# Three six-tile passes instead of four in a second network, with preparation work moved earlier

## The chip, the cores and the metric

The kernel runs on one core of a Trainium2 chip. The time is device microseconds for one execution. Three runs of the kernel before took 825.73 to 828.0 us, median 827.82 us.

## What is computed

Sparse attention (4 batches, 8 heads, 576 tokens, head size 64) gives 2304 tokens of 512 numbers. They go through a gated layer of eight experts, each token through one, and then through a second network that is the same for all tokens:

```python
h = np.maximum(x[mask] @ w1[e], 0.0)            # 512 -> 1024, per expert
out[mask] = gate_w[mask, None] * eom[mask, e, None] * (h @ w2[e])
...
h = np.maximum(x @ w_in, 0.0)                   # 512 -> 2048, all tokens
return (h * h @ w_out).astype(np.float32)       # 2048 -> 512
```

`w_in` and `w_out` arrive as float64, so the kernel must turn pairs of 32-bit words into float32 itself.

## The kernel before

**Every product is made of three.** Each float32 matrix is split into a high part (a copy rounded to fp32r, on ScalarE) and a low part (the difference, on VectorE). `mm3` (L936 to 939) multiplies high by high (L937) and the two mixed pairs (L938, L939; which line is which depends on the order of the arguments) into the same PSUM tile. In names an h stands for high and an l for low: `hw`/`lw` are weights of the experts, `xh`/`xl` tokens, `hh`/`hl` hidden values of an expert, `gh`/`gl` hidden values of the second network, `hwa`, `hwb`, `hwo` and `lwa`, `lwb`, `lwo` its weights.

**Stages.** Attention and routing end 180 us into the span. Then come eight experts, k = 0 to 7, with 416 tokens at first and 256 at last. Each has eight steps f. Step f makes one hidden block `h` (`e_l1`, 12 matmuls) and, two steps later, adds that block to the four output tiles `y` (`e_l2`, 12 matmuls). After step 7 ScalarE copies the four `y` into `y2T` (L1060), which holds the inputs of the second network. VectorE makes `hl` at L1037.

**The second network** goes over the 18 token tiles (128 tokens each) in passes. A pass with two halves uses seven products instead of eight per 256 hidden columns: `m_unit` forms products of combined weights (A11, A12, A22, S1 to S4; rows show m_0A and m_0S for unit 0) with sums of token blocks (B11, T1 to T4 and so on, made by `split2` in four parts, 0 to 3; its rows are L1082 `xt`, `xs` and L1066 `xh`/`xl`/`xbl`). Each product goes to one of only two PSUM buffers, and VectorE empties it: L1239 makes a running sum `u`, L1157 a sum `rl`. ScalarE then does Relu (L1159), Square (L1160) and the high part (L1065), VectorE the low part `gl` (L1066). `down` multiplies these by `hwo`/`lwo` into six output tiles `o`; `quarters` hands out that work in four pieces, which `m_unit` puts between the next unit's products. After the last unit of a pass each tile `o` is scaled (L1183 or L1185) and written by GpSimd as a scatter to `out` (L1186). Before, the passes cover 6, 6, 4 and 2 tiles; the last one has one half and uses `m_plain` (L937 rows `m<-xh,hwi`), with plain blocks of the weights.

**Conversion of float64.** `conv` (L184 to 198) takes 128 x 512 pairs: ScalarE takes the absolute value of the high word (L184), VectorE shifts and masks it (L186, L187) and scales the low word (L191, output `cvd`), GpSimd adds the two (L192, output `cvt`), VectorE puts the sign back (L198). It runs 16 times for `w_in` during the experts (tiles `e6`, `eo`; L993 then makes the combined weights `sa`, `sb`, which GpSimd writes to `ws_d`) at steps listed in `CONV`, and 16 times for `w_out` inside the first pass (loads `s0wo`, `s1wo`, result `rwo`).

**What sets the order.** The kernel is written in program order, and a scheduler with its own time estimates reorders instructions of each engine. On the chip each engine then takes its own list strictly in that order, so an instruction that waits holds up all that stand behind it.

The lines the change touches:

Of the kernel before, what the change touches and what calls it, by code (L numbers as in the profile page):

```python
# [7 lines left out]
F32 = mybir.dt.float32  # L8
# [3 lines left out]
U32 = mybir.dt.uint32  # L12
AF = mybir.ActivationFunctionType
ALU = mybir.AluOpType
# [6 lines left out]
P = 128  # L21
NT = B * S
D = H * HD
KD = D // P
E = 8
# [34 lines left out]
C0 = LATE * P // E  # L60
HB = 8

MG = [(3, 3), (3, 3), (2, 2), (2,)]
LPOOL = (13, 14, 15, 16, 17)
DS = 6
LN = 6
# [10 lines left out]
BLK = {n: i for i, n in enumerate("A21 A11 A22 A12 S1 S2 S3 S4".split())}  # L77
BW = 2 * P

CONV = [(k, f) for k in range(1, 8) for f in range(8)][2:-6]  # L80
NW = (max(CAPS) + P - 1) // P
NEG = -1.0e9

# [48 lines left out]
def moe_kernel(ctx, tc, q, k, v, wg, wog, w1, w2, w_in64, w_out64, consts, out, dbg=None):  # L132
# [48 lines left out]
    def conv(pool, raw, o, nm, parts_=False):  # L181
        hi, lo = raw[:, :, 1], raw[:, :, 0]
        n = hi.shape[1]
        nc.scalar.activation(o, hi.bitcast(F32), AF.Abs)  # L184
        t = pool.tile([P, n], I32, name=f"cvt{nm}", tag="cvt")
        nc.vector.tensor_scalar(t, hi, 3, 0x3FFFFFFF, op0=ALU.logical_shift_left, op1=ALU.bitwise_and)  # L186
        nc.vector.scalar_tensor_tensor(  # L187
            out=t, in0=hi, scalar=-0x40000000, in1=t, op0=ALU.bitwise_and, op1=ALU.bitwise_or
        )
        rd = pool.tile([P, n], I32, name=f"cvd{nm}", tag="cvd", bufs=1)  # L190
        nc.vector.tensor_scalar(rd, lo.bitcast(U32), 2.0**-29, None, op0=ALU.mult)  # L191
        nc.gpsimd.tensor_tensor(t, t, rd, op=ALU.add)  # L192
        if parts_:
            return t
        conv_end(t, o)
# [662 lines left out]
    raws = early[0]  # L858
    for g in range(len(MG)):
        for c in range(F2 // UC):  # L860
            units += [("wa", g, c), ("wb", g, c), ("wo", g, c)] if len(MG[g]) == 2 else [("wi", g, c), ("wo", g, c)]
    ready = {}
    nraw = [1]
    nwh = [-1]
# [2 lines left out]
    def prep_unit(u):  # L867
        kind, k, c = u
        cs = slice(c * UC, (c + 1) * UC)
        if kind == "w1":  # L870
            shp = [P, KD, UC]
        elif kind in ("wa", "wi"):
            shp = [P, 4, BW]
        elif kind == "wb":
            shp = [P, 3, BW]
        else:
            shp = [P, UC // P, D]
# [7 lines left out]
        if kind == "w1":  # L885
            src = w1[bass.ds(order_of(k), 1), :, cs].rearrange("e (a p) f -> p (e a) f", p=P)
        elif kind == "w2":
            src = w2[bass.ds(order_of(k), 1), cs, :].rearrange("e (a p) f -> p (e a) f", p=P)
        elif kind == "wi":
            src = ws_d[c, :, : 4 * BW].rearrange("p (b f) -> p b f", f=BW)  # L890
        elif kind == "wa":
            src = ws_d[c, :, BW : 5 * BW].rearrange("p (b f) -> p b f", f=BW)
        elif kind == "wb":
            src = ws_d[c, :, 5 * BW :].rearrange("p (b f) -> p b f", f=BW)
        else:
            src = wout_d[cs, :].rearrange("(a p) f -> p a f", p=P)
# [144 lines left out]

    ybk = {}

    def e_l2(k, f, hh, hl):
        C = CAPS[k]
        c, i = f * P // UC, f % (UC // P)
        wh, wl = get(("w2", k, c))
        if f == 0:
            ybk[k] = [psm.tile([P, 512], F32, name=f"y{k}_{d}", tag="a", bufs=6) for d in range(KD)]
        for d in range(KD):  # L1050
            ds_ = slice(d * P, (d + 1) * P)
            mm3(
                ybk[k][d][:, :C], wh[:, i, ds_], wl[:, i, ds_], hh[:, :C], hl[:, :C], f == 0, f == NF1 - 1
            )
        if f == NF1 - 1:
            off = 0
            if k:
                off = nc.values_load(meta[0:1, E + k : E + k + 1], engines=[ET.Activation], min_val=0, max_val=NT)
            for d in range(KD):
                nc.scalar.activation(y2T[:, d, bass.ds(off, C)], ybk[k][d][:, :C], AF.Copy)  # L1060
# [7 lines left out]
    def split2(g, part):  # L1068

        c0, HC = sum(map(sum, MG[:g])) * P, MG[g][0] * P  # L1070
        if len(MG[g]) == 1:
            if part == 0:
                xh, xl = x_tiles(f"2{g}")
                half_split(y2T[:, :, c0 : c0 + HC], xh[:, :, :HC], xl[:, :, :HC])
                x2[g] = (xh, xl)
            return
        if part == 0:
            x2[g] = {}
        X = x2[g]
# [36 lines left out]
    for k in range(E):  # L1116
        for f in range(NF1):
            h = e_l1(k, f)
            if len(pend) == 2:
                e_l2(*pend.pop(0))  # L1120
            pend.append((k, f) + h)
            if f == 1 and k + 1 < E:
                if k == 0:
                    ixs[1] = rows_of(1, order_of(1))
                win_load(k + 1)
                if k + 2 < E:
                    ixs[k + 2] = rows_of(k + 2, order_of(k + 2))
            if (k, f) == (0, 1):
                with tc.issue_after(lead["win"].ins) if MSW else nullcontext():
                    nc.gpsimd.memset(y2T, 0.0)  # L1130
            if (k, f) == (0, 1):
                places()
            if (k, f) >= PLACES and puts:
                puts.pop(0)()
            conv_done()
            if (k, f) in CONV:
                n = CONV.index((k, f))
                if n == 0:
                    conv_load(0)
                    conv_load(1)  # L1140
                for j in range(n * len(halves) // len(CONV), (n + 1) * len(halves) // len(CONV)):
                    conv_early(j)
            if f == 4 and k + 1 < E:
                win_split(k + 1)
            if k == E - 1 and f in (2, 4):
                split2(0, (f - 2) // 2)
    while pend:
        e_l2(*pend.pop(0))
    split2(0, 2)
    split2(0, 3)  # L1150

# [16 lines left out]
    def down(g, f, ts, t00, hs, first, last):  # L1168
# [6 lines left out]
        for t in ts:  # L1175
            t0 = (t - t00) * P
            mm3(obk[g][t], hh[:, t0 : t0 + P], hl[:, t0 : t0 + P], wh[:, i, :], wl[:, i, :], first, last)
            if last:
# [13 lines left out]
                if g + t:  # L1192
                    tc.declare_no_dep(ins.ins, group="rows", reason="rows of different tokens differ")
                tc.add_to_no_dep_group("rows", ins.ins)

    def m_plain(g, f):
        HC = MG[g][0] * P
        c, i = f * P // UC, f % (UC // P)
        ahead(("wi", g, c), 5)
        wh, wl = get(("wi", g, c))  # L1200
        xh, xl = x2[g]
        ps = psm.tile([P, 512], F32, name=f"m{g}_{f}", tag="h", bufs=2)
        for a in range(KD):
            b, s_ = a // 2 * 2 + i, slice(a % 2 * P, (a % 2 + 1) * P)
            mm3(ps[:, :HC], wh[:, b, s_], wl[:, b, s_], xh[:, a, :HC], xl[:, a, :HC], a == 0, a == KD - 1)
        return squared(f"{g}_{f}", ps, HC)

    def quarters(g, c, hs):

# [54 lines left out]
        q()  # L1264
        return quarters(g, c, hs)

    todo = iter(())
    for g in range(len(MG)):
        if len(MG[g]) == 2:
            for c in range(F2 // UC):  # L1270
                todo = m_unit(g, c, todo)
            continue
        pend = []
        for f in range(NF2):
            pend.append((f, m_plain(g, f)))
            for w in todo:
                w()
            if f:
                f0, h = pend.pop(0)
                down(g, f0, range(MG[g][0]), 0, h, f0 == 0, False)  # L1280
        f0, h = pend.pop(0)
        down(g, f0, range(MG[g][0]), 0, h, False, True)
    bulk.close()


# [136 lines left out]
```

## Time and profile before

| | before |
|---|---|
| median of 3 runs | 827.82 us |
| the profiled execution, its own time | 829.9 us |
| its span | 828.1 us |
| TensorE busy, instructions | 775.9 us (94%), 5331 matmuls |
| VectorE busy | 578.8 us (70%) |
| ScalarE busy | 495.7 us (60%) |
| GpSimd busy | 215.4 us (26%) |
| granted TensorE clock, mean | 0.975 |

Busy times are sums over the whole span and hide the stages. A matmul's own duration overlaps its successor's, so what one matmul costs in a full stream is read from start to start. A row of a timeline gives start, duration, engine, line, operation, output and inputs; in brackets behind it is the idle time just before and who ended it. In a table of windows the number after each engine is its busy time in that stretch.

### The profile page before, as it was taken

The numbers are of one execution on the slowest core, as the hardware profiler recorded it, in microseconds if no ns is written. First come the engines' busy times: TensorE is split into PE (matmuls) and PEld (weight loads), VectorE is DVE, ScalarE is ACT, GpSimd is POOL, SyncE is SP. The second block draws the span as 40 slices with busy tenths as digits, with TensorE's granted clock in tenths as the row PEclk, the third lists the DMA queues.
The fourth block names the chain that finished last, engine by engine and source line by source line (L and its number), as shares of the span: only waits on it lengthen the run. The fifth ranks groups of instructions, "written<-read, shape, count | busy, mean of one in ns | idle before, by whom it ended". The sixth has DMA issues, their size and how long they took to land.

```text
span 828.1 us, 14972 instructions
## 1 busy us (share of the span) xinstructions
PE 775.9 (94%) x5331; PEld 716.2 (86%) x5331; DVE 578.8 (70%) x1174; ACT 495.7 (60%) x1230; POOL 215.4 (26%) x210
## 2 busy tenths in 40 slices
PE   4999799789999999999979999999999999999995
PEld 3898788689999999999877788888898898998994
DVE  4677567466457687788998998787565577667651
ACT  2878568515444545556555755676564577767862
POOL 7213133437054754322133322003000003000200
PEclk9999979779999999999999999999999999999998
DMA  8987801429758899877445553425223225444620
GB/s 170 185 179 158 178 14 53 140 94 302 228 159 236 199 284 275 262 253 271 160 155 179 176 216 122 140 96 172 80 89 113 70 89 197 140 140 153 200 82 30
DMA packets 110022, 133.28 MB, mean 161 GB/s; under 512 B 43057, under 2 KB 77393, under 8 KB 109938
## 3 DMA queue, kind: packets, MB, share of 16 engines
q1 hardware_dynamic: 100354, 109.16, 46.1%
q0 software_dynamic: 8096, 22.63, 7.6%
q8 instruction: 44, 0.72, 0.4%
q10 hardware_dynamic: 1488, 0.44, 0.3%
q14 instruction: 40, 0.33, 0.2%
HBM read 110.08 MB, written 22.12 MB: 160 GB/s over the span
## 4 chain that ended last, share of the span: by engine, by line
PE 29%; issue 20%; DVE 7%; DMA 3%; ACT 3%; POOL 1%; DVEq 0%; POOLq 0%; ACTq 0%; SPq 0%
PE o L937 3%; PE o L938 3%; PE o L939 3%; PE h L937 2%; PE y L938 2%; PE y L939 2%; PE h L939 2%; PE h L938 2%; PE y L937 2%; DMA s0wo<-in_moe_w_out_dram 2%; DVE gl L1066 1%; DMA s1wo<-in_moe_w_out_dram 1%; DVE rl L1157 1%; POOL out_dram L1186 1%; DVE cvtwo L187 1%
## 5 line engine op out<-in xcount | busy, mean ns | idle before, releaser
L937 PE MATMUL o<-hwo,gh 128*128 128x512 f32 x288 | 114.4, 399 | 3.5 <-ACT gh L1065 3.4
L921 DVE TENSOR_TENSOR lw<-rw,hw 128x1024 fp32r<-128x1024 f32 x62 | 79.1, 1276 | 49.7 <-ACT hw L917 41.8
L938 PE MATMUL o<-lwo,gh 128*128 128x512 f32 x288 | 113.8, 396 | 0.0
L917 ACT ACTIVATE hw<-rw 128x1024 fp32r<-128x1024 f32 x62 | 65.9, 1062 | 77.5 <-PE h L938 40.9
L1159 ACT ACTIVATE rl<-rl 128x384 f32<-128x384 f32 (+1 forms) x96 | 45.9, 482 | 84.5 <-DVE rl L1157 83.8
L1186 POOL DMA_INDIRECT out_dram<-ob,idx x18 | 21.0, 1165 | 275.7 <-ACT ob L1185 271.4
L939 PE MATMUL o<-hwo,gl 128*128 128x512 f32 x288 | 86.1, 395 | 1.3 <-DVE gl L1066 1.3
L1066 DVE TENSOR_TENSOR gl<-rl,gh 128x384 fp32r<-128x384 f32 (+1 forms) x112 | 58.7, 531 | 35.5 <-ACT gh L1065 34.7
L937 PE MATMUL h<-xh,hw 128*128 128x416 f32 (+7 forms) x256 | 81.0, 316 | 2.7 <-DVE hl L1037 2.7
L939 PE MATMUL h<-xh,lw 128*128 128x416 f32 (+7 forms) x256 | 79.6, 311 | 0.0
L938 PE MATMUL h<-xl,hw 128*128 128x416 f32 (+7 forms) x256 | 79.5, 310 | 0.0
L938 PE MATMUL y<-hl,hw 128*128 128x416 f32 (+7 forms) x256 | 76.6, 310 | 0.0
L939 PE MATMUL y<-hh,lw 128*128 128x416 f32 (+7 forms) x256 | 76.2, 310 | 0.0
L937 PEld LDWEIGHTS o<-hwo,gh 128*128 128x128 f32 x288 | 54.2, 188 | 14.2 <-ACT gh L1065 5.5
L937 PE MATMUL y<-hh,hw 128*128 128x416 f32 (+7 forms) x256 | 65.3, 311 | 0.0
L938 PEld LDWEIGHTS o<-lwo,gh 128*128 128x128 f32 x288 | 54.5, 189 | 8.8
L939 PEld LDWEIGHTS o<-hwo,gl 128*128 128x128 f32 x288 | 52.6, 188 | 11.0 <-DVE gl L1066 1.7
L1065 ACT ACTIVATE gh<-rl 128x384 fp32r<-128x384 f32 (+1 forms) x112 | 53.0, 475 | 2.1
L1160 ACT ACTIVATE rl<-rl 128x384 f32<-128x384 f32 (+1 forms) x112 | 52.5, 472 | 1.9
L937 PEld LDWEIGHTS h<-xh,hw 128*128 128x128 f32 x256 | 48.2, 188 | 4.1 <-DVE hl L1037 3.9
L938 PEld LDWEIGHTS h<-xl,hw 128*128 128x128 f32 x256 | 48.2, 188 | 0.3 <-DVE xl L632 0.2
L939 PEld LDWEIGHTS h<-xh,lw 128*128 128x128 f32 x256 | 48.1, 188 | 0.1
(611 smaller groups left out, 2178.7 us busy)
## 6 DMA issues: line engine op xcount, KB each, us to landing
rw<-in_moe_w_dram SPq DMA_DIRECT2D x62, 512.0 KB
rwa<-ws_d SPq DMA_DIRECT2D x24, 512.0 KB
rwo<-wout_d SPq DMA_DIRECT2D x24, 512.0 KB
rwb<-ws_d SPq DMA_DIRECT2D x24, 384.0 KB
e6wi<-in_moe_w_in_dram SPq DMA_DIRECT2D x32, 256.0 KB
x_d<-xr SPq DMA_DIRECT2D x18, 256.0 KB
ws_d<-eo POOLq DMA_DIRECT2D x16, 256.0 KB
s0wo<-in_moe_w_out_dram SPq DMA_DIRECT2D x8, 512.0 KB
```

The costliest lines, as they stand in the source:

```text
L187: nc.vector.scalar_tensor_tensor(out=t, in0=hi, scalar=-0x40000000, in1=t, op0=ALU.bitwise_and, op1=ALU.bitwise_or)
L917: nc.scalar.activation(hi, raw, AF.Copy)
L921: eng.tensor_tensor(lo, raw, hi.bitcast(F32), op=ALU.subtract)
L937: nc.tensor.matmul(ps, ah, bh, start=first, stop=False)
L938: nc.tensor.matmul(ps, ah, bl_, start=False, stop=False)
L939: nc.tensor.matmul(ps, al, bh, start=False, stop=last)
L1065: nc.scalar.activation(h, x, AF.Copy)
L1066: nc.vector.tensor_tensor(l, x, h.bitcast(F32), op=ALU.subtract)
L1157: nc.vector.tensor_tensor(rl[:, :HC], src, add, op=ALU.add)
L1159: nc.scalar.activation(rl[:, :HC], src, AF.Relu)
L1160: nc.scalar.activation(rl[:, :HC], rl[:, :HC], AF.Square)
L1186: ins = nc.gpsimd.indirect_dma_start(out=out[:, :], out_offset=bass.IndirectOffsetOnAxis(ap=idx[:, gt_, 0:1], axis=0), in_=ob, in_offset=None,
```

## The change

- `MG`, the list of passes, becomes three passes of two halves with three tiles each; `m_plain` and all that only the two-tile pass used is gone.
- `CONV` starts one step earlier and ends eight steps earlier: the sixteen conversions of `w_in` are spread over 41 steps (experts 1 to 6) instead of 48.
- The low word's scaling (L191) goes from VectorE to ScalarE, for all 32 conversions.
- `split2(0, 0)` and `split2(0, 1)` are called at step 5 of expert 6 and step 0 of expert 7, not at steps 2 and 4 of expert 7.
- The last two blocks of expert 7 (`e_l2`) are no longer made ahead of the second network but handed in four pieces to its first `m_unit`.

```diff
-MG = [(3, 3), (3, 3), (2, 2), (2,)]
+MG = [(3, 3), (3, 3), (3, 3)]
...
-CONV = [(k, f) for k in range(1, 8) for f in range(8)][2:-6]
+CONV = [(k, f) for k in range(1, 8) for f in range(8)][1:-14]
...
-        nc.vector.tensor_scalar(rd, lo.bitcast(U32), 2.0**-29, None, op0=ALU.mult)
+        nc.scalar.activation(rd, lo.bitcast(U32), AF.Copy, scale=2.0**-29)
...
-    def e_l2(k, f, hh, hl):
+    def e_l2(k, f, hh, hl, ds=range(KD)):
...
-        for d in range(KD):
+        for d in ds:
...
-        if f == NF1 - 1:
+        if f == NF1 - 1 and KD - 1 in ds:
...
-            if k == E - 1 and f in (2, 4):
-                split2(0, (f - 2) // 2)
-    while pend:
-        e_l2(*pend.pop(0))
+            if (k, f) in ((E - 2, 5), (E - 1, 0)):
+                split2(0, k + 2 - E)
     split2(0, 2)
     split2(0, 3)
...
-    todo = iter(())
+    todo = iter([lambda a=a, d=d: e_l2(*a, range(d, d + 2)) for a in pend for d in (0, 2)])
     for g in range(len(MG)):
-        if len(MG[g]) == 2:
-            for c in range(F2 // UC):
-                todo = m_unit(g, c, todo)
-            continue
-        pend = []
...
+        for c in range(F2 // UC):
+            todo = m_unit(g, c, todo)
+    for w in todo:
+        w()
```

Line numbers of the changed kernel are 2 to 32 lower in this part of the code (L919 for L921, L1217 for L1239, L1176 for L1186).

VectorE's list where the second network begins, before, up to the first sum of unit 0 (`u_0`, made from the product of S2):

```order
L1037 SCALAR_TENSOR_TENSOR hl_7_5737<-h_7_5723,hh_7_5736 128x256
L186 TENSOR_SCALAR cvtwo_0_1_5682<-s1wo_0_5679 128x512
L1066 TENSOR_TENSOR xl_2_5791<-xt_5539,xh_2_5790 128x768
L187 SCALAR_TENSOR_TENSOR cvtwo_0_1_5682<-s1wo_0_5679,cvtwo_0_1_5682 128x512
L921 TENSOR_TENSOR lwb_1_5818<-rwb_1_5814,hwb_1_5816 128x768
L198 SCALAR_TENSOR_TENSOR rwo_0_5668<-rwo_0_5668,cvtwo_0_0_5672 128x512
L191 TENSOR_SCALAR cvdwo_0_1_5685<-s1wo_0_5679 128x512
L1082 TENSOR_TENSOR xs_2_0_5794<-y2T 128x384
L1239 TENSOR_TENSOR u_0_5821<-m_0S_5832,u_0_5820 128x384
L1082 TENSOR_TENSOR xs_2_0_5794<-xs_2_0_5794,xt_5539 128x384
L1066 TENSOR_TENSOR xbl_5805<-y2T,xbh_5804 128x768
L1157 TENSOR_TENSOR rl_0_10_5847<-m_0A_5840,u_0_5820 128x384
```

And the same place of the change:

```order
L1035 SCALAR_TENSOR_TENSOR hl_7_5737<-h_7_5723,hh_7_5736 128x256
L1064 TENSOR_TENSOR xl_2_5753<-xt_5340,xh_2_5752 128x768
L1064 TENSOR_TENSOR xl_2_5753<-xs_2_0_5756,xh_2_5752 128x384
L1064 TENSOR_TENSOR xl_2_5753<-xs_2_1_5761,xh_2_5752 128x384
L919 TENSOR_TENSOR lwb_1_5780<-rwb_1_5776,hwb_1_5778 128x768
L186 TENSOR_SCALAR cvtwo_1_0_5913<-s0wo_1_5910 128x512
L186 TENSOR_SCALAR cvtwo_1_1_5923<-s1wo_1_5920 128x512
L919 TENSOR_TENSOR lwa_1_5774<-rwa_1_5770,hwa_1_5772 128x1024
L1217 TENSOR_TENSOR u_0_5783<-m_0S_5794,u_0_5782 128x384
L187 SCALAR_TENSOR_TENSOR cvtwo_1_0_5913<-s0wo_1_5910,cvtwo_1_0_5913 128x512
L187 SCALAR_TENSOR_TENSOR cvtwo_1_1_5923<-s1wo_1_5920,cvtwo_1_1_5923 128x512
L1074 TENSOR_TENSOR xt_6953<-y2T 128x768
```

Before, token sums (`xs_2_0`, `xbl`) stand between the sums that empty PSUM. In the change part 2 of `split2` is complete ahead of `u_0`, and the conversion rows there belong to the next block of `w_out`.

ScalarE's list behind the last copy into `y2T`, in the change:

```order
L1058 ACTIVATE y2T<-y_3_5550 128x256
L191 ACTIVATE cvdwo_1_1_5926<-s1wo_1_5920 128x512
L1149 ACTIVATE rl_0_10_5815<-rl_0_10_5815 128x384
L1150 ACTIVATE rl_0_10_5815<-rl_0_10_5815 128x384
L1063 ACTIVATE gh_0_10_5819<-rl_0_10_5815 128x384
L191 ACTIVATE cvdwo_2_0_6085<-s0wo_2_6079 128x512
L1149 ACTIVATE rl_0_01_5844<-rl_0_01_5844 128x384
```

The two `cvdwo` rows are new on this engine, and they stand ahead of the Relu of a hidden block.

GpSimd's last writes of the result, before (the end of the four-tile pass, then the two-tile pass):

```order
L1186 DMA out_dram<-ob_3_9469,idx 2304x512
L1186 DMA out_dram<-ob_0_9933,idx 2304x512
L1186 DMA out_dram<-ob_1_9939,idx 2304x512
```

and in the change (the end of the second pass, then the last one):

```order
L1176 DMA out_dram<-ob_5_8470,idx 2304x512
L1176 DMA out_dram<-ob_0_9489,idx 2304x512
L1176 DMA out_dram<-ob_1_9495,idx 2304x512
L1176 DMA out_dram<-ob_2_9501,idx 2304x512
L1176 DMA out_dram<-ob_3_9507,idx 2304x512
L1176 DMA out_dram<-ob_4_9513,idx 2304x512
L1176 DMA out_dram<-ob_5_9519,idx 2304x512
```

Six writes, not two, stand behind the last matmuls.

## Rows read from the trace of the kernel before

**Rows 1.** The page: VectorE's share and TensorE's granted clock in 40 equal slices.

```profile
DVE  4677567466457687788998998787565577667651
PEclk9999979779999999999999999999999999999998
```

**Rows 2.** Windows (stretch, its length, then busy time of PE, PEld, DVE, ACT, POOL; clock).

```profile
180.30:403.00 222.70, 221.75 (x1495) 219.48 (x1494) 156.28 (x268) 114.75 (x189) 92.24 (x85) 1.00 0.79 238
355.00:379.00 24.00, 24.00 (x188) 23.80 (x187) 19.15 (x32) 12.39 (x23) 5.32 (x7) 1.00 0.84 278
403.00:439.00 36.00, 29.67 (x186) 26.46 (x184) 33.69 (x58) 17.70 (x34) 10.70 (x8) 0.95 0.43 147
439.00:545.00 106.00, 102.50 (x499) 89.70 (x500) 94.67 (x149) 67.48 (x121) 24.25 (x20) 1.00 0.48 165
545.00:560.00 15.00, 13.77 (x68) 11.91 (x67) 12.94 (x23) 12.60 (x23) 0.00 (x0) 1.00 0.25 74
685.00:770.00 85.00, 84.09 (x519) 75.07 (x519) 60.70 (x118) 61.16 (x129) 6.97 (x6) 1.00 0.47 152
```

**Rows 3.** Waits of TensorE from 400 to 560 us (total, times, longest).

```profile
PE o L937 <- ACT gh L1065: 3.4, 4, 1.9
...
PE m_0S L937 <- DVE rl L1157: 1.1, 1, 1.1
```

**Rows 4.** Timeline at the second product of the second network.

```profile
422.13 0.33 PE L939 MATMUL m_0S<-xh,lwb 128*128 128x384 f32 x1
...
423.41 0.55 DVE L1239 TENSOR_TENSOR u<-m_0S,u 128x384 f32<-128x384 f32 x1
...
424.01 0.45 PE L937 MATMUL m_0S<-xh,hwb 128*128 128x384 f32 x1 [0.50 <-DVE u L1239]
```

**Rows 5.** Timeline in the first pass: GpSimd's addition beside VectorE.

```profile
449.82 1.94 POOL L192 TENSOR_TENSOR cvtwo<-cvtwo,cvdwo 128x512 int32<-128x512 int32 x1 [4.05 <-DVE cvdwo L191]
...
450.53 1.77 DVE L198 SCALAR_TENSOR_TENSOR rwo<-rwo,cvtwo 128x512 f32<-128x512 f32 x1
...
452.82 0.96 PE L939 MATMUL o<-hwo,gl 128*128 128x512 f32 x3 [1.26 <-DVE gl L1066]
```

**Rows 6.** Timeline: first and last of 12 matmuls 384 wide, of 11 matmuls 256 wide.

```profile
447.90 0.34 PE L937 MATMUL m_1S<-xh,hwa 128*128 128x384 f32 x1
...
449.83 0.34 PE L939 MATMUL m_1A<-xh,lwa 128*128 128x384 f32 x1
...
773.50 0.28 PE L937 MATMUL m<-xh,hwi 128*128 128x256 f32 x1
...
774.70 0.28 PE L938 MATMUL m<-xl,hwi 128*128 128x256 f32 x1
```

**Rows 7.** Groups of VectorE from 403 to 439 us (busy us, mean ns).

```profile
L1066 DVE TENSOR_TENSOR xl<-xs,xh 128x384 fp32r<-128x384 f32 x6 | 3.2, 548 | 0.0
...
L1082 DVE TENSOR_TENSOR xs<-y2T,xt 128x384 f32<-128x384 f32 x2 | 2.2, 1102 | 0.0
L1082 DVE TENSOR_TENSOR xs<-y2T 128x384 f32<-128x384 f32 x4 | 2.2, 545 | 0.0
...
L1066 DVE TENSOR_TENSOR xl<-y2T,xh 128x768 fp32r<-128x768 f32 x2 | 1.9, 944 | 0.0
```

**Rows 8.** Groups of the whole span: low word on VectorE, absolute value on ScalarE.

```profile
L184 ACT ACTIVATE eo<-e6wi 128x512 f32<-128x512 f32 x16 | 10.8, 673 | 0.0
...
L191 DVE TENSOR_SCALAR cvde<-e6wi 128x512 int32<-128x512 uint32 x16 | 6.9, 430 | 0.0
```

**Rows 9.** Timeline at the end: last matmuls and GpSimd's writes.

```profile
817.14 0.63 PE L939 MATMUL o<-hwo,gl 128*128 128x512 f32 x2
...
818.53 0.97 POOL L1186 DMA_INDIRECT out_dram<-ob,idx  x1 [37.11 <-ACT ob L1185]
819.80 0.96 POOL L1186 DMA_INDIRECT out_dram<-ob,idx  x1 [0.30 <-issue]
```

**Rows 10.** Wait of ScalarE for loads, 400 to 560 us (total, times, longest).

```profile
ACT rwo L184 <- DMA s1wo<-in_moe_w_out_dram: 2.4, 2, 1.2
```

More of the change, by code (lines that the diff above doesn't have):

```diff
@@ L860, in moe_kernel @@
         for c in range(F2 // UC):
-            units += [("wa", g, c), ("wb", g, c), ("wo", g, c)] if len(MG[g]) == 2 else [("wi", g, c), ("wo", g, c)]
+            units += [("wa", g, c), ("wb", g, c), ("wo", g, c)]
     ready = {}
@@ L871, in prep_unit @@
             shp = [P, KD, UC]
-        elif kind in ("wa", "wi"):
+        elif kind == "wa":
             shp = [P, 4, BW]
@@ L888, in prep_unit @@
             src = w2[bass.ds(order_of(k), 1), cs, :].rearrange("e (a p) f -> p (e a) f", p=P)
-        elif kind == "wi":
-            src = ws_d[c, :, : 4 * BW].rearrange("p (b f) -> p b f", f=BW)
         elif kind == "wa":
@@ L1070, in split2 @@
         c0, HC = sum(map(sum, MG[:g])) * P, MG[g][0] * P
[L1071 to L1076, printed above, removed]
         if part == 0:
@@ L1194, in down @@
                 tc.add_to_no_dep_group("rows", ins.ins)
[L1196 to L1206, printed above, removed]
     def quarters(g, c, hs):
@@ L1265, in m_unit @@
         return quarters(g, c, hs)
-    todo = iter(())
+    todo = iter([lambda a=a, d=d: e_l2(*a, range(d, d + 2)) for a in pend for d in (0, 2)])
     for g in range(len(MG)):
-        if len(MG[g]) == 2:
-            for c in range(F2 // UC):
-                todo = m_unit(g, c, todo)
-            continue
-        pend = []
[L1274 to L1282, printed above, removed]
+        for c in range(F2 // UC):
+            todo = m_unit(g, c, todo)
+    for w in todo:
+        w()
     bulk.close()
```

## The prediction

> **What bounds the kernel now.** I read the page's 40 slices first [rows 1]: from about 180 us on the granted TensorE clock is at its full level nearly everywhere, and VectorE's share climbs from the fifteenth slice and stands at eight and nine tenths from the nineteenth to the twenty-fifth, which is the end of the experts and the first pass of the second network. Then I cut the span into stages [rows 2]. TensorE is busy for 221.75 of the 222.7 us of experts 0 to 6 and the start of 7, and for 84.09 of 85 us around the end of the second pass. There it is the bound, and only fewer or shorter matmuls help. Between 403 and 439 us it is busy for 29.67 of 36 us while VectorE is busy for 33.69, and the clock's mean is 0.95. So at the change from experts to second network VectorE is the bound: TensorE idles 6.3 us, and 0.05 x 36 = 1.8 us more go to a short spell at the lower of its two levels (1.2 GHz) behind those idle stretches. That is 8.1 us. In the rest of the first pass, 439 to 545 us, TensorE idles 3.5 us, and VectorE is busy for 94.67 of 106.
>
> The list of waits says the same [rows 3]: TensorE waits for ScalarE's `gh` (3.4 us) and for VectorE's sums. The timeline shows the mechanism [rows 4]: the product of S2 issues its last matmul at 422.13, but VectorE starts to empty its PSUM buffer only at 423.41, since it was behind with its list, and the next product that needs that buffer starts at 424.01. With two buffers, every late sum becomes a TensorE wait.
>
> **The passes.** The four-tile and the two-tile pass go, one six-tile pass comes. `down` does the same 18 tiles either way. The products: before, 8 x 42 = 336 matmuls and 16 x 12 = 192 matmuls, all 256 wide; now 336 of 384. From start to start a 256-wide one takes (774.70 - 773.50)/10 = 0.120 us and a 384-wide one (449.83 - 447.90)/11 = 0.1755 us [rows 6]. So 528 x 0.120 = 63.4 becomes 336 x 0.1755 = 59.0: **-4.4 us**, all on TensorE where it is the bound. The eight loads and splits of plain blocks and eight of `w_out` that go with the fourth pass lie beside TensorE work there and count nothing; in a six-tile pass without conversions TensorE is not held up, so no new cover is lost.
>
> **The end.** Before, two writes stand behind the last matmuls, now six. GpSimd starts one 819.80 - 818.53 = 1.27 us after another and the last takes 0.96 [rows 9]. The first can start about 1.0 us after its tile is done (TensorE's second-last matmul ends near 817.5, the write starts at 818.53). In the order of the change the first of six tiles is done eleven matmuls before the end; at 0.23 us each (the pair at 817.14 lasts 0.63 with 0.4 of its own drain [rows 9]) that is 2.5 us ahead. The sixth write then ends 5 x 1.27 + 0.96 - 1.5 = 5.8 us after the last matmul, against 3.0 before: **+2.8 us** (bounds +1.5 if tiles come out earlier, +4 if VectorE's scaling delays them).
>
> **The change of networks.** Out of VectorE's 403 to 439 us go the token sums of parts 0 and 1 [rows 7]: four of the six `xl<-xs` (2.2), both `xl<-y2T` (1.9), both `xs<-y2T,xt` (2.2), two of the four `xs<-y2T` (1.1); and low words at 0.43 each [rows 8], four of them (1.7). That is 9.1 of 33.69 us. What stays, 24.6, stands against some 28 us of TensorE at full clock. The order shows no token sum left between the sums that empty PSUM. I take 6 of the 8.1 us: **-6.0**. At least 0 would go if other waits take their place (below), at most 8.1. The four pieces of expert 7's last blocks I cost at nothing: both lists already had the first product between those blocks, so this part does little that the scheduler had not done.
>
> **The rest of the first pass.** VectorE loses a low word for each of 13 conversions, 5.6 of 94.67 us. That is about half of what it needs to be as free as in the later passes; I take **-1.8** of the 3.5 us (0 to -3.5). ScalarE gains as many. The trace has no low word on ScalarE; the nearest row is the absolute value of as many words at 0.673 us against 0.430 on VectorE [rows 8]. 13 x 0.673 = 8.7, so ScalarE goes from 67.48 to about 76 of 106 us [rows 2]: cover enough if nothing waits in its list. The Trainium skill, ScalarE: Activation LUTs, Rules for kernel authors, says that multiplications belong on VectorE and not on ScalarE; by that rule the move costs time, and the two rows agree that the instruction itself gets longer.
>
> **Experts 6 and 7.** Parts 0 and 1 land mostly in expert 6. It has 24 us, VectorE 19.15 of them busy [rows 2]. The sums add three 768 wide (0.94) and eight 384 wide (0.55), 7.2 us; about two conversions fewer run there, each four steps of VectorE like the low word's 0.43 [rows 8] or somewhat longer, so 4 us go at most. That makes 22 to 24 of 24. One late `hl` there costs TensorE a wait: **+1.0** (0 to +3). The conversions per step rise from 16/48 to 16/41 in experts whose VectorE share is 156.28/222.7 = 70%: nothing. The boundary of two passes idles 1.2 us at 545 to 560 and 0.9 at the second [rows 2]; the second becomes like the first: **+0.3**.
>
> **The sum** is -4.4 + 2.8 - 6.0 - 1.8 + 1.0 + 0.3 = -8.1 us against the profiled execution's 829.9, so 821.8. That execution is 2.1 us above the median of 827.82; in terms of the medians I forecast **819.7 us**.
>
> **Rivals.**
>
> *The waits stay (826.5).* GpSimd's addition L192 remains in all 32 conversions, and while it runs VectorE's own instructions stretch: a sign step of 512 elements beside it took 1.77 us, and TensorE then waited 1.26 us for `gl` [rows 5]; of sums of one shape, two take 1.10 us in the mean where four take 0.55 [rows 7]. If the remaining waits come from that and not from VectorE's load, the two middle terms shrink to about -1, and the sum is -4.4 + 2.8 - 1 + 1.3 = -1.3. For it: sixteen such additions stay in the first pass. Against: the wait in rows 4 came on a stretch where VectorE was late by its list. The rule behind this mechanism is in the Trainium skill, SBUF — State Buffer, Who interferes with whom: a VectorE instruction with two SBUF inputs and a GpSimd instruction that reads SBUF lock each other out; by that rule alone the low word's move (one input) would free nothing of the lock, and rows 5 agree with it.
>
> *ScalarE's list becomes the wait (831).* Each low word now needs its load on the engine that also makes Relu, Square and `gh`, and it stands ahead of them. ScalarE already waited 1.2 us twice for such a load [rows 10], and TensorE's longest waits are for its `gh` [rows 3]. If each of the 16 conversions of `w_out` holds it 1.2 + 0.67 us and a third reaches TensorE, that is +10, and the 1.8 is not gained: 819.7 + 11.8 = 831.5. It decides once a conversion holds ScalarE for more than its slack, (106 - 76)/13 = 2.3 us. Against it: ScalarE's mean load stays near 72%.
>
> *Deeper (814).* All of the 8.1 and 3.5 us go, and expert 6 costs nothing: -4.4 + 2.8 - 8.1 - 3.5 + 0.3 = -12.9, so 815; with the end at its lower bound 814.
>
> **How the numbers follow.** About 0.3%, 2.5 us, is what a measurement of this kernel can tell from no change: 825.3 to 830.3. My forecast has 0.58 (817 to 825), deeper 0.13, the waits that stay 0.18 (a third of it just faster), ScalarE 0.09 (a little of it still the same), something else 0.02. Faster 0.78, same 0.14, slower 0.08. The range of 813 to 827 leaves out ScalarE's case and the outer tenth of the others.
>
> **What would show it.** Right: in the window of the last expert's end TensorE idles under 3 us with the clock at 1.00; no wait of a product for `u` or `rl` of unit 0 over 0.5 us; 528 products of 256 columns replaced by 336 of 384, and a stretch after the last matmul that is about 3 us longer. Wrong: TensorE waits for `gh` behind a low word on ScalarE; a new idle stretch in expert 6 that ends with `hl`; or idle time in the first pass as large as before beside stretched VectorE instructions.

## The result, and the profile after

| | before | after |
|---|---|---|
| median | 826.23 us (20 runs, 822.46 to 831.6) | 819.04 us (20 runs, 815.25 to 830.71) |
| after / before | | 0.9917 (95%: 0.9892 to 0.9942) |
| the profiled execution | 829.9 us | 815.72 us |
| its span | 828.1 us | 813.9 us |

The change is faster by 7.2 us in the medians; 8.1 were forecast. The two profiled executions stand 14.2 us apart, because 6.7 us of that lie ahead of the experts: attention and routing end at 180.4 us in one and at 173.7 us in the other. Nothing is changed there. In the twelve profiles of the experiments that point lies anywhere between 172.1 and 180.4 us. So stretches behind it are compared, each from the first matmul of one stage to the first of the next (the last two meet at the start of the last matmul):

| stretch | before | after | difference | forecast |
|---|---|---|---|---|
| experts 0 to 5 | 187.05 | 187.34 | +0.3 | 0 |
| expert 6 | 25.08 | 26.17 | +1.1 | +1.0 |
| expert 7 and first pass | 160.13 | 152.24 | -7.9 | -7.8 |
| the other passes, to the last matmul | 264.72 | 261.38 | -3.3 | -4.1 |
| behind the last matmul | 10.72 | 12.99 | +2.3 | +2.8 |
| sum | | | -7.5 | -8.1 |

These are the page's slices of after. VectorE's share in slices 19 to 25, 8998998 in [rows 1], is now 9889777.

```profile
DVE  4778578565467578779889777787654687566442
PEclk9999989779999999999999999999999999999998
```

Windows of after (the columns are those of [rows 2]): the 36 us that lie to the first pass as 403 to 439 us did, and expert 7 with the whole first pass.

```profile
394.50:430.50 36.00, 33.14 (x227) 30.73 (x227) 31.04 (x49) 26.21 (x48) 11.42 (x8) 1.00 0.52 170
387.24:539.48 152.24, 146.49 (x809) 131.92 (x808) 123.03 (x195) 106.51 (x192) 30.78 (x24) 1.00 0.47 159
```

At the change of networks TensorE idles 2.9 us where it idled 6.3, and its clock stays at the full level. Over expert 7 and the first pass VectorE has 123.0 us of work in 152.2 where the kernel before has this:

```profile
392.52:552.65 160.13, 149.90 (x808) 133.03 (x807) 143.34 (x228) 99.08 (x180) 37.51 (x30) 0.99 0.46 159
```

What a later VectorE does to ScalarE is seen in ScalarE's own waits over this stretch (total, times, longest). Before:

```profile
ACT rl L1159 <- DVE rl L1157: 37.8, 13, 6.8
```

After:

```profile
ACT rl L1149 <- DVE rl L1147: 15.8, 13, 2.8
ACT cvdwo L191 <- POOL cvtwo L192: 11.4, 7, 3.3
ACT cvdwo L191 <- DMA s0wo<-in_moe_w_out_dram: 7.8, 4, 2.6
```

ScalarE waits 22 us less for VectorE's sums. In their place it waits 7.8 us for the load of its low words, and 11.4 us for GpSimd: the low word's output `cvd` has one buffer (`bufs=1`), and ScalarE can't write the next one before GpSimd has added the last.

TensorE's waits of after in the same stretch answer to [rows 3]:

```profile
PE o L937 <- DVE gl L1064: 2.0, 3, 0.9
PE o L935 <- ACT gh L1063: 1.7, 3, 0.8
PE m_0S L935 <- DVE rl L1147: 1.2, 1, 1.2
PE h L935 <- DVE hl L1035: 0.4, 1, 0.4
PE m_0S L935 <- DVE u L1217: 0.4, 1, 0.4
```

The end answers to [rows 9]: the last matmuls, then six writes of GpSimd.

```profile
799.69 0.97 POOL L1176 DMA_INDIRECT out_dram<-ob,idx  x1 [113.19 <-ACT ob L1175]
...
800.39 0.86 PE L937 MATMUL o<-hwo,gl 128*128 128x512 f32 x3
...
806.06 0.97 POOL L1176 DMA_INDIRECT out_dram<-ob,idx  x1 [0.30 <-issue]
```

### The profile page after: what moved, and what is told of

Read it like the earlier page. It is cut to its first block, busy times and chain, and to the rows that moved or that the text cites. A ratio compares the mean times of both kernels' runs of the same rounds, so it can differ in the third digit from the quotient of the medians.

```text
span 813.9 us, 14424 instructions
## 1 busy us (share of the span) xinstructions
PE 763.5 (94%) x5139; PEld 704.9 (87%) x5139; DVE 553.9 (68%) x1109; ACT 493.3 (61%) x1197; POOL 216.8 (27%) x210
## 4 chain that ended last, share of the span: by engine, by line
PE 55%; issue 17%; DMA 9%; DVE 7%; ACT 6%; POOL 4%; SPq 1%; POOLq 0%; ACTq 0%; DVEq 0%
DMA s0wo<-in_moe_w_out_dram 4%; PE o L935 4%; PE h L935 4%; PE o L936 4%; PE o L937 4%; PE y L935 4%; PE y L936 3%; PE h L936 3%; PE y L937 3%; PE h L937 3%; PE rw L481 2%; DMA ks<-in_k_dram 1%; DMA rw<-in_moe_w_dram 1%; POOL win L520 1%; PE lr L622 1%
## 5 line engine op out<-in xcount | busy, mean ns | idle before, releaser
L919 DVE TENSOR_TENSOR lw<-rw,hw 128x1024 fp32r<-128x1024 f32 x62 | 78.2, 1262 | 43.2 <-ACT hw L915 42.6
L1149 ACT ACTIVATE rl<-rl 128x384 f32<-128x384 f32 x96 | 49.5, 519 | 94.9 <-DVE rl L1147 94.8
L1176 POOL DMA_INDIRECT out_dram<-ob,idx x18 | 20.6, 1147 | 275.5 <-ACT ob L1175 271.0
L1064 DVE TENSOR_TENSOR gl<-rl,gh 128x384 fp32r<-128x384 f32 x96 | 56.8, 593 | 44.3 <-ACT gh L1063 43.2
L937 PE MATMUL o<-hwo,gl 128*128 128x512 f32 x288 | 83.6, 396 | 2.0 <-DVE gl L1064 2.0
L935 PE MATMUL y<-hh,hw 128*128 128x416 f32 (+7 forms) x256 | 68.0, 311 | 0.4 <-ACT hh L1034 0.4
L937 PEld LDWEIGHTS o<-hwo,gl 128*128 128x128 f32 x288 | 53.6, 188 | 12.8 <-DVE gl L1064 3.0
L1063 ACT ACTIVATE gh<-rl 128x384 fp32r<-128x384 f32 x96 | 49.9, 521 | 1.8
L1150 ACT ACTIVATE rl<-rl 128x384 f32<-128x384 f32 x96 | 49.6, 519 | 1.7
L936 PEld LDWEIGHTS y<-hl,hw 128*128 128x128 f32 x256 | 48.1, 188 | 0.1
```

Source lines behind the costliest of these rows:

```text
L919: eng.tensor_tensor(lo, raw, hi.bitcast(F32), op=ALU.subtract)
L935: nc.tensor.matmul(ps, ah, bh, start=first, stop=False)
L936: nc.tensor.matmul(ps, ah, bl_, start=False, stop=False)
L937: nc.tensor.matmul(ps, al, bh, start=False, stop=last)
L1063: nc.scalar.activation(h, x, AF.Copy)
L1064: nc.vector.tensor_tensor(l, x, h.bitcast(F32), op=ALU.subtract)
```

## The experiments

The sum was right. Whether its terms were is what the runs were for. **Theory:** VectorE is relieved where it was late, mostly by the token sums (the larger part of the -6.0, in which four low words count too), the low words adding -1.8. **Rivals:** the low words are the larger part; the denser conversions cost something; ScalarE or GpSimd take over the wait. Twelve kernels, each compared with the kernel before on its chip. "Spell" is time at the lower clock level (1.2 GHz) in expert 7 and the first pass.

| kernel | ratio to before (95%) | experts 1 to 6 | expert 7, first pass | spell | to last matmul | behind it | span x clock, us |
|---|---|---|---|---|---|---|---|
| before | 1 | 178.2 | 160.1 | 3.4 | 264.7 | 10.7 | 0 |
| after | 0.9917 (0.9892 to 0.9942) | 179.7 | 152.2 | 0 | 261.4 | 13.0 | not on record |
| passes alone | 1.0000 (0.9963 to 1.0038) | 178.3 | 159.3 | 3.4 | 261.5 | 13.0 | -2.7 |
| low words alone | 0.9954 (0.9922 to 0.9987) | 177.4 | 157.3 | 6.8 | 264.8 | 11.1 | -5.7 |
| conversions alone | 1.0053 (1.0025 to 1.0082) | 181.3 | 159.2 | 6.8 | 264.7 | 10.8 | -0.2 |
| passes and low words | 0.9954 (0.9921 to 0.9987) | 180.4 | 156.6 | 3.4 | 261.4 | 12.6 | -5.3 |
| all but the passes | 0.9931 (0.9883 to 0.9979) | 180.2 | 152.6 | 0 | 264.8 | 11.1 | -3.1 |
| all but the low words | 0.9995 (0.9961 to 1.0029) | 187.0 | 153.4 | 0 | 261.3 | 12.6 | -0.1 |
| all but the token sums | 0.9905 (0.9858 to 0.9951) | 178.3 | 155.6 | 6.8 | 261.4 | 12.9 | -7.2 |
| all but the blocks | 0.9933 (0.9899 to 0.9967) | 179.0 | 154.3 | 6.8 | 261.4 | 12.6 | -6.5 |
| all but the conversions | 0.9927 (0.9891 to 0.9962) | 177.3 | 159.0 | 6.8 | 261.5 | 12.7 | -6.2 |
| low words left out | 0.9838 (0.9783 to 0.9893) | 179.1 | 148.4 | 0 | 261.5 | 12.6 | -11.8 |
| low words twice | 0.9968 (0.9929 to 1.0006) | 180.6 | 155.4 | 0 | 261.6 | 12.8 | -3.0 |
| tiles in turn | 0.9936 (0.9907 to 0.9965) | 180.4 | 151.8 | 0 | 261.5 | 11.1 | -7.0 |

A stretch is that of one profiled execution. Where two kernels have the same lists it repeats mostly to 0.2 us, but not in experts 2 and 3: these hold up to 3 us of waits in single profiles, for most of which the trace names no cause (low words alone: 177.4; with the passes, which are changed only later: 180.4).

The last column takes the clock out. Half of the time at the lower level is lost where TensorE is the bound, and most of that loss lies in attention and routing, where nothing is changed: between 8.5 and 18.8 us in the fourteen profiles. The record has the span and the mean granted clock of each execution; their product is an estimate of the span without that loss (a step of the rounded clock is worth 0.8 us), and over the twenty executions of after its standard deviation is 1.4 us where that of the span is 4.6. The column gives its median less that of before on the same chip; a 95% interval reaches 1 to 3 us to either side. For the runs of before beside after no clocks are on record.

### Passes alone (the kernel before, edited)

```diff
-MG = [(3, 3), (3, 3), (2, 2), (2,)]
+MG = [(3, 3), (3, 3), (3, 3)]
...
         down(g, f0, range(MG[g][0]), 0, h, False, True)
+    for w in todo:
+        w()
```

> The kernel before with the three six-tile passes alone; conversions, low words, token sums and last expert blocks stay where they were. My sum: -4.4 us of matmuls, +0.3 at the boundary of passes, +2.3 to +2.8 behind the last matmul, nothing between the start of expert 7 and the second pass (160.1 us there in the kernel before, 152.2 in the changed one): about -1.5 us in all, second pass to last matmul 261 us where it was 264.7, 13.0 us behind the last matmul where it was 10.7. If the passes carry the whole gain (rival), -7 us in all and the stretch from expert 7 to the second pass shortens too.

A ratio of 1.0000 with an interval of 3 us to either side settles nothing by itself. The stretches do: in the ten profiles with three passes the way from the second pass to the last matmul takes 261.3 to 261.6 us, in the four with four passes 264.7 or 264.8. That is -3.3. Behind the last matmul it is 12.6 to 13.0 us in nine of the ten (the tenth has the tiles in turn) against 10.7 to 11.1, some +1.8. The passes are worth about -1.5 us in all.

### All but the passes (after, with four passes and the plain pass restored)

```diff
-MG = [(3, 3), (3, 3), (3, 3)]
+MG = [(3, 3), (3, 3), (2, 2), (2,)]
...
```

> The changed kernel with the old passes of 6, 6, 4 and 2 tiles. My sum: expert 7 to second pass 152 us (the whole 7.9 us stays), expert 6 takes 26.2 us instead of 25.1, second pass to last matmul 264.7 and 10.7 us behind it: about -6 us in all. If the passes carry the gain: no faster than before.

0.9931: the gain is there without the passes, and their stretches are those of before.

### All but the low words (after, edited)

```diff
-        nc.scalar.activation(rd, lo.bitcast(U32), AF.Copy, scale=2.0**-29)
+        nc.vector.tensor_scalar(rd, lo.bitcast(U32), 2.0**-29, None, op0=ALU.mult)
```

> The changed kernel with the low word back on VectorE. My sum gives the low words 1.7 us at the change of networks and 1.8 us in the rest of the first pass: expert 7 to second pass 154 to 156 us where the changed kernel takes 152.2. If VectorE's load there does not matter any more after the token sums are gone (rival): 152 us and the same time. If ScalarE's list is what still holds up the first pass (rival): shorter, 150 us.

The miss that turned the study: with this line alone put back the whole gain is gone (0.9995, and -0.1 us in the last column). That is 6.4 us by the ratios, and the interval does not touch that of after. The loss is not where the sum had put it. Expert 7 and the first pass lose only 1.2 us; experts 1 to 6 lose 7.3.

### All but the token sums (after, edited)

```diff
-            if (k, f) in ((E - 2, 5), (E - 1, 0)):
-                split2(0, k + 2 - E)
+            if k == E - 1 and f in (2, 4):
+                split2(0, (f - 2) // 2)
```

> The changed kernel with the two token sums called in expert 7 as before. My theory gives them most of the gain: expert 7 to second pass 156 to 158 us instead of 152.2, and expert 6 back at 25.1 us instead of 26.2, so some 4 us slower than the changed kernel. If it is the conversions of w_in, gone from expert 7, that made room (rival): 152 to 153 us, and faster than the changed kernel by the 1.1 us of expert 6.

The theory lost its main term: 0.9905, no slower than after, where 4 us were expected (a ratio of 0.9966). In the profile the sums do cost expert 7 and the first pass 3.4 us, the spell included, and give 1.6 back in expert 6.

### All but the blocks (after, edited)

```diff
             if (k, f) in ((E - 2, 5), (E - 1, 0)):
                 split2(0, k + 2 - E)
+    while pend:
+        e_l2(*pend.pop(0))
     split2(0, 2)
     split2(0, 3)
```

> The changed kernel with expert 7's last blocks put ahead of the rest of the token sums again, as they were before. My theory costs this part of the change at nothing, since TensorE's order hardly differs: the time is that of the changed kernel within 1.5 us (819 to 820), and expert 7 together with the first pass takes 152 us as there. Rival, the deferred blocks are what covers VectorE's late sums at the change of networks: then 3 to 5 us come back, and TensorE waits for sums of unit 0 again.

0.9933 is not told apart from after. The profiled stretch is 2.1 us longer, between the two expectations, with a spell of 6.8 us, which at half clock costs 3.4.

### All but the conversions, and conversions alone

```diff
-CONV = [(k, f) for k in range(1, 8) for f in range(8)][1:-14]
+CONV = [(k, f) for k in range(1, 8) for f in range(8)][2:-6]
```

> The changed kernel with the conversions back over the 48 steps up to expert 7, low words still on ScalarE and the token sums in expert 6. Theory one, VectorE's room at the change of networks comes from the conversions that no longer run in expert 7: expert 7 and the first pass go from 152 to about 156 us, experts 0 to 6 stay near 213, and the time is 823 to 824. Theory two, the low words on ScalarE alone make that room (three steps of 0.43 us are left where there were four): expert 7 and the first pass stay within 1.5 us of 152, and the time is 819 to 821.

The time (0.9927) is that of theory two, the stretch (159.0) worse than either said: conversions in expert 7 do hold TensorE up, by 6.8 us in this profile, 3.4 of them from its spell, and 2.4 are given back in experts 1 to 6. The rest isn't seen in the median; one profile and a median with this interval cannot decide it.

The other way round, the kernel before with `[1:-14]`:

> The kernel before with one other line of the change: the conversions spread over 41 steps from expert 1 to expert 6 where 48 steps reached into expert 7; low words stay on VectorE, token sums stay in expert 7. If denser conversions cost VectorE what the run with low words on VectorE suggests (experts 0 to 6 took 220.9 there against 213.5 us), experts 0 to 6 take 217 to 220 us here against 212.1 before, expert 7 and the first pass go from 160 to 155 to 157, and the time is no better than before, 826 to 830. If denser conversions cost nothing, as my prediction had it, experts 0 to 6 stay at 212 to 214 us and the time is 822 to 824.

Slower than before by 0.5%: of the three parts that were run alone the only one that does harm. Experts 1 to 6 lose 3.0 us and expert 4 more than that, 33.17 us where it takes 28.50 before. The timeline of that place:

```profile
312.31 0.65 ACT L184 ACTIVATE eo<-e6wi 128x512 f32<-128x512 f32 x1
...
313.21 1.27 POOL L837 DMA_DIRECT2D idx<-idx_d  x1 [4.45 <-DMA idx_d<-toki,cpi]
...
314.50 1.28 POOL L192 TENSOR_TENSOR cvte<-cvte,cvde 128x512 int32<-128x512 int32 x1
315.81 0.69 DVE L198 SCALAR_TENSOR_TENSOR eo<-eo,cvte 128x512 f32<-128x512 f32 x1 [4.78 <-POOL cvte L192]
316.42 0.49 DVE L1037 SCALAR_TENSOR_TENSOR hl<-h,hh 128x328 fp32r<-128x328 f32 x1
...
316.96 0.41 PE L937 MATMUL h<-xh,hw 128*128 128x304 f32 x1 [2.74 <-DVE hl L1037]
```

Read it from the top. GpSimd is to fetch the table of token indices (L837) and stands 4.45 us until the scattered writes of that table have landed. Its addition for a conversion is queued behind. VectorE stands idle for 4.78 us before the step that needs the addition, and `hl` is queued behind that. TensorE waits 2.74 us for `hl`. So VectorE isn't overloaded here; a list is held up by a transfer that has nothing to do with it. Then the clock falls:

```profile
317.40:320.80 3.40, 3.40 (x15) 3.40 (x14) 3.40 (x9) 0.91 (x1) 0.41 (x2) 0.50 0.62 214
```

With the two spells of its first pass that makes three of 3.4 us, where before has one. In the last column the kernel is level with before (-0.2), so what it loses over its executions it loses to the clock: 4.7 us more than before in the median (1.7 to 8.5). Two more spells make 3.4 of that in this profile; the rest can lie in attention, which the edit does not touch.

The kernel with all but the low words has the same at the same step, here with the same order of L837 ahead of L192:

```profile
315.59 1.27 POOL L837 DMA_DIRECT2D idx<-idx_d  x1 [4.89 <-DMA idx_d<-toki,cpi]
316.88 1.28 POOL L192 TENSOR_TENSOR cvte<-cvte,cvde 128x512 int32<-128x512 int32 x1
318.20 0.69 DVE L198 SCALAR_TENSOR_TENSOR eo<-eo,cvte 128x512 f32<-128x512 f32 x1 [3.92 <-POOL cvte L192]
...
319.36 0.45 PE L935 MATMUL h<-xh,hw 128*128 128x304 f32 x1 [1.89 <-DVE hl L1035]
```

A spell of 3.4 us follows here too, worth 1.7. Expert 4 takes that kernel 3.45 us longer than after. After differs from it in one line only, and in its list an addition stands ahead of the fetch and none directly behind it:

```profile
303.75 1.29 POOL L192 TENSOR_TENSOR cvte<-cvte,cvde 128x512 int32<-128x512 int32 x1
...
307.57 1.30 POOL L837 DMA_DIRECT2D idx<-idx_d  x1 [2.53 <-DMA idx_d<-toki,cpi]
```

GpSimd waits there too (2.53 us), but no conversion is held up. Before, an addition did stand behind the fetch, but GpSimd's wait was 2.69 us and TensorE's work covered it. Of the 7.3 us that "all but the low words" loses in the experts this explains a half; 3.2 lie in expert 2, in waits for which no view names a releaser, and stay open; a second spell of 3.4 us follows them.

### Low words alone, and with the passes (the kernel before, edited)

```diff
-        nc.vector.tensor_scalar(rd, lo.bitcast(U32), 2.0**-29, None, op0=ALU.mult)
+        nc.scalar.activation(rd, lo.bitcast(U32), AF.Copy, scale=2.0**-29)
```

> The kernel before with one line of the change: low words on ScalarE, all else as it was. Theory two, the low words are the larger part of the gain: expert 7 and the first pass go from 160 to about 154 us, and the time is 820 to 822. Theory one, and my prediction's sum (-1.8 us for the low words, of which part lies after the change of networks): 158 us for that stretch and 824 to 826. If ScalarE's list were the wait, the stretch would get longer than 160.

0.9954, or 0.0046 x 825 = 3.8 us, and -3.7 us in the two stretches of the table: one line is worth half of the change by the medians (1.1 to 6.4 us), and in the last column (-5.7) most of it. Even so a wait takes the place of those removed:

```profile
PE o L937 <- ACT gh L1065: 2.8, 5, 0.8
PE m_0A L937 <- ACT xh L1065: 2.4, 1, 2.4
```

The first product of unit 0 waits 2.4 us for `xh`, the rounding of token sums, which still stand at steps 2 and 4 of expert 7. In the windows there ScalarE and VectorE are both full, TensorE then runs at half clock:

```profile
417.30:421.30 4.00, 1.57 (x7) 1.02 (x7) 4.00 (x7) 3.84 (x7) 0.33 (x1) 0.99 0.35 131
421.30:428.10 6.80, 6.27 (x18) 5.57 (x18) 6.33 (x12) 2.50 (x5) 0.90 (x1) 0.50 0.43 139
```

That is the wait which the earlier token sums remove. With the passes as well:

> The kernel before with two parts of the change only: three six-tile passes and the low words on ScalarE. Conversions stay over 48 steps, token sums stay in expert 7, the last blocks stay ahead. If the runs so far add up (low words alone -3.8 us in experts and first pass, passes alone -1), the time is 4 to 6 us below before, and within 1.5 us of the changed kernel's ratio of 0.9917: then the other three parts are worth almost nothing together. My prediction's sum (passes -1.3 with the end, low words -1.8, change of networks -6.0 from token sums and conversions) gives only -3 us or less here, a ratio of 0.996.

The ratio is 0.9954 once more, and the wait of 2.4 us for `xh` is there again. The intervals of this kernel and of after overlap, so that the three other parts are worth nothing is neither shown nor excluded; the stretch of expert 7 and first pass is 4.3 us longer than in after.

### Low words left out, and made twice (after, edited)

```diff
-        rd = pool.tile([P, n], I32, name=f"cvd{nm}", tag="cvd", bufs=1)
-        nc.scalar.activation(rd, lo.bitcast(U32), AF.Copy, scale=2.0**-29)
-        nc.gpsimd.tensor_tensor(t, t, rd, op=ALU.add)
```

> The changed kernel without the low words at all: neither ScalarE's step nor GpSimd's addition, so the output loses the lowest bits of the converted weights. Rival from the prediction, the waits left in expert 7 and the first pass come from GpSimd's addition, beside which VectorE's steps stretch: then steps of the form of L186 and L187 are back at 0.42 and 0.68 us in the mean, and expert 7 with the first pass goes from 152.2 to 149 or less. Theory, what is left there is mostly ScalarE's gh and the order of the lists: 151 to 152 us, and the time within 1.5 us of the changed kernel's.

0.9838 (four runs) and 148.4 us in the stretch: the rival "the waits stay" lives on in what is left. Groups of VectorE in that stretch (busy us, mean ns), first after:

```profile
L1064 DVE TENSOR_TENSOR gl<-rl,gh 128x384 fp32r<-128x384 f32 x29 | 19.6, 680 | 7.7 <-ACT gh L1063 7.2
...
L186 DVE TENSOR_SCALAR cvtwo<-s1wo 128x512 int32<-128x512 int32 x8 | 4.1, 516 | 0.0
```

then without low words and GpSimd's additions (line numbers are 3 lower there):

```profile
L1061 DVE TENSOR_TENSOR gl<-rl,gh 128x384 fp32r<-128x384 f32 x29 | 16.1, 554 | 9.1 <-ACT gh L1060 8.4
...
L186 DVE TENSOR_SCALAR cvtwo<-s1wo 128x512 int32<-128x512 int32 x8 | 3.4, 424 | 2.0 <-DMA s1wo<-in_moe_w_out_dram 1.9
```

With no additions beside them on GpSimd the same instructions are 126 and 92 ns shorter, and TensorE's 2.0 us for `gl` are gone. The Trainium skill, SBUF — State Buffer, Who interferes with whom, has VectorE and GpSimd share one pair of ports under a lock; the `gl` rows (two SBUF inputs) agree. L186 has one input and stretches too, which the page allows only in its two-port modes: 424 ns for 512 elements, where L187 with two inputs takes 684 for as many, would fit one, but no run here shows the mode. `L191` on VectorE has one input too and took 0.43 us for 512 elements, so the prediction's reading, that its move would free nothing of the lock, is not safe. The kernel also leaves out ScalarE's step, so its 3.9 us are not GpSimd's alone.

```diff
         nc.scalar.activation(rd, lo.bitcast(U32), AF.Copy, scale=2.0**-29)
+        nc.scalar.activation(rd, lo.bitcast(U32), AF.Copy, scale=2.0**-29)
```

> The changed kernel with each low word made twice on ScalarE (0.68 us more for each of 32 conversions, 22 us of ScalarE in all). If ScalarE has the slack that my prediction gave it (2.3 us per conversion in the first pass), expert 7 with the first pass stays at 152 to 153.5 us and the time within 1.5 us of the changed kernel's. If ScalarE's list is already what TensorE waits for, half of the doubled cost or more shows: 16 x 0.68 / 2 = 5 us in that stretch, and as much again in experts 1 to 6.

The stretch grows by 3.2 us, between the two expectations: 16 x 0.67 = 10.7 us more on ScalarE, and a third of it shows there. Experts 1 to 6 grow by 0.9. The median says 0.9968 against 0.9917 (+4.2 us, intervals overlapping). In the last column it is -3.0 (-4.8 to -1.6) against -7.0 (-8.3 to -5.4) of the tiles in turn on the same chip, which differ from after only at the end. So ScalarE is not off the path.

### Tiles in turn (after, edited)

The second and third of the last unit's four pieces change places, and `issue_after` keeps the last two behind the matmul issued before them, so that the scheduler can't mix them:

```diff
-        nc.tensor.matmul(ps, al, bh, start=False, stop=last)
+        lead["mm"] = nc.tensor.matmul(ps, al, bh, start=False, stop=last)
...
+        if c == F2 // UC - 1 and g == len(MG) - 1:
+            hs[1], hs[2] = hs[2], hs[1]
         return quarters(g, c, hs)
...
-    for w in todo:
-        w()
+    for n, w in enumerate(todo):
+        with tc.issue_after(lead["mm"].ins) if n > 1 else nullcontext():
+            w()
```

> The changed kernel with the last unit's four pieces in another order, so that the first three token tiles are finished nine matmuls before the other three, where all six now come within twelve matmuls. GpSimd's six writes start 1.27 us apart; started nine matmuls of 0.23 us earlier, the last would end some 2 us earlier: 10.9 us behind the last matmul of the second product instead of 13.0, and a ratio near 0.989. If the writes wait for something else than their tiles (scaling on VectorE, GpSimd's list), the stretch stays at 12.5 to 13.

The last matmuls and the first and last write of GpSimd:

```profile
803.24 0.97 POOL L1176 DMA_INDIRECT out_dram<-ob,idx  x1 [111.38 <-DVE ob L1173]
...
805.75 0.86 PE L937 MATMUL o<-hwo,gl 128*128 128x512 f32 x3
...
809.76 0.97 POOL L1176 DMA_INDIRECT out_dram<-ob,idx  x1 [0.30 <-issue]
```

The stretch behind the last matmul is 11.05 us, where 10.9 was expected: writes that start earlier end earlier, and the edit gives 1.9 us back. The ratio, 0.9936, cannot show so little; that this version beats after is not shown.

## Why the prediction was right, and where not

**The time and its total were right.** -8.1 us was forecast, -7.2 measured in the medians and -7.5 in the stretches. That the total came so close is in part luck: as told below, the token sums were priced too high and the low words too low, and what denser conversions do to the lists and the clock had no price.

**The passes** gave -3.3 with the second boundary, not -4.1. Over all 720 matmuls of 256 columns in the trace before and all 1020 of 384 after, the medians from start to start are 0.118 and 0.174 us, so the products gain 62.3 - 58.5 = 3.8 and not 4.4; the row with 0.120 was a little slow. **The end:** the last matmul ends at 800.39 + 0.86 = 801.25 and the sixth write at 806.06 + 0.97 = 807.03, 5.8 us behind it, exactly as reckoned against 3.0 before. That the stretch grew by 2.3 and not by 2.8 lies behind the last write: 7.3 us to the end of the span before, 6.8 after. **Expert 6** lost 1.1 us, and one late `hl` costs TensorE 0.8 us there, as described.

**The step that failed** is the weighing of the two middle terms, and the place where they act. Behind "I take 6 of the 8.1 us" stood 9.1 us of VectorE's work, 7.4 of token sums and 1.7 of low words, so in proportion -4.9 and -1.1; with "-1.8 of the 3.5 us" the low words had -2.9. The sum of -7.8 was met (-7.9). But the token sums, called late again, cost that stretch 3.4 us and give 1.6 back in expert 6: 1.8 net where 4.9 - 1.0 = 3.9 was reckoned, and the median shows no loss at all. What they remove is one wait of 2.2 to 2.4 us. The low words give about -3.8 alone, and without them the rest of the change is worth nothing measurable; most of what is lost with them shows in experts 1 to 6 (7.3 us in one profile, 3.2 of them unexplained), for which the sum had no such term.

Nor was VectorE left with "24.6" us of work in the 36 us at the change of networks. The window above has 31.04, since splits of weights and conversions that stood later moved into the room. TensorE's idle time fell from 6.3 to 2.9 us all the same. So VectorE was freed less than reckoned there; that its new order, without the token sums ahead of the sums that empty PSUM, did the rest is likely, but no run separates order from amount.

**A second step failed unseen:** "The conversions per step rise from 16/48 to 16/41 ...: nothing." True with the low words on ScalarE (179.7 against 178.2 us, 1.1 of it the token sums in expert 6), false without (181.3 alone, and 0.5% slower). I priced VectorE's share, 70%, and not what stands behind a waiting instruction on GpSimd. The change is right as a whole because one part pays for another.

**The blocks** at nothing: not contradicted by the median, 2.1 us in one profile; open.

**The rivals.** "The waits stay" did not happen, but names what is left. "ScalarE's list becomes the wait" did not decide, but its threshold of 2.3 us slack per conversion was wrong: 0.67 us more each already cost 3.2 in the stretch. "Deeper" did not happen: 2.9 us of idle time stay at the change of networks, and expert 6 did cost. ScalarE's low word takes 0.68 us, as the nearest row had it, and the Trainium skill, ScalarE: Activation LUTs, Rules for kernel authors, which puts multiplications on VectorE, is right about the instruction's length (0.68 us against 0.43); the measurement decides for ScalarE here.

**The signs that the prediction named:** TensorE idles 2.9 us at the change of networks at full clock, as said; a wait for `rl` of unit 0 of 1.2 us is still there, which it had ruled out. Of its signs of being wrong, the idle stretch in expert 6 that ends with `hl` is there (0.8 us), and so, twice, is a wait for `gh` behind a low word on ScalarE (0.55 and 0.79 us). The first of them:

```profile
419.94 0.68 ACT L191 ACTIVATE cvdwo<-s1wo 128x512 int32<-128x512 uint32 x1 [3.34 <-POOL cvtwo L192]
...
421.62 0.52 ACT L1063 ACTIVATE gh<-rl 128x384 fp32r<-128x384 f32 x1
...
422.20 0.50 PE L935 MATMUL o<-hwo,gh 128*128 128x512 f32 x1 [0.55 <-ACT gh L1063]
```

ScalarE stood 3.34 us before this low word until GpSimd was done with the one `cvd`, and Relu, Square and `gh` followed it closely. The rival named the right list; at this size it did not decide.

Open is how GpSimd's addition and ScalarE's step share the 3.9 us of what the low words still cost. A second buffer for `cvd`, which would free ScalarE of its 11.4 us of waits for GpSimd, was not tried.

## What to carry to other kernels

A step moved from the fullest engine to a freer one, even if it gets longer there, can be what makes the other moves affordable. Try each part of a change alone, and the change without each part, before crediting one. Look at the lists of engines that seem idle, too: an instruction that waits for a transfer on GpSimd held VectorE and then TensorE for one that had nothing to do with it.

## What the runs showed of the hardware that was not expected

The clock made the price of a wait uneven. In all eight kernels that lack at least one of earlier conversions, earlier token sums and deferred blocks, TensorE ran 3.4 or 6.8 us at half clock (1.2 GHz) in expert 7 or the first pass: in seven of them behind single idle pieces of 1.95 to 2.85 us, in one behind two of 0.8 and 1.5 us. In the six kernels that have the three it kept the full level there, with single pieces of 1.05 to 1.53 us at most. A single spell of 6.8 us costs 3.4 us, more than the wait ahead of it. It is no rule: with the low words twice, a wait of 2.3 us in expert 3 had no spell behind it, and with the low words on VectorE two of 1.1 and 0.85 us in expert 2 had one. Whether other executions had these spells is open: the medians of the three kernels that lack only one part can't show 3.4 us, with intervals of 3 to 4 us to either side and 8.5 to 18.8 us lost to the clock ahead of the experts.
